# Pooled attention with a top-1 mixture of experts: the first batch's keys loaded and summed another way, score groups on two banks of their own in the first four tiles, weights' low parts on GpSimd, and a new table of order

## The chip, the cores and the metric

The kernel runs on one core of one Trainium2 chip. A core has a matrix engine (PE, TensorE), a vector engine (DVE, VectorE), an activation engine (ACT, ScalarE), GpSimd (POOL), a queue engine that issues most transfers (SP), and 16 DMA engines. Matrix results go to PSUM, which has eight banks of 512 float32 columns on 128 partitions here; everything else lies in SBUF. Each engine takes its instructions strictly in the order in which the program lists them. The metric is the device time of one execution, in microseconds (us).

## The reference

Four batches of 12,288 queries of 128 channels, and four images of 384 x 32 pixels of 128 channels. The image is averaged over 4 x 4 pixels, giving 768 positions, and projected; the result is both key and value. Attention over the 768 keys gives 128 channels per query, and each query then goes through one of eight experts, the one with the greatest gate logit.

```python
kv_pool = kv.reshape(B, H // r, r, W // r, r, C).mean(axis=(2, 4))     # r = 4
k = v = kv_pool.reshape(B, -1, C) @ w_sr
s = 1.0 / np.sqrt(C) * (q @ k.transpose(0, 2, 1))
a = np.exp(s - s.max(-1, keepdims=True))
a /= a.sum(-1, keepdims=True) + 1e-09
x = (a @ v)                                                   # then, per token:
logits = x @ w_gate;  expert_idx = argmax(logits);  gate_w = softmax(logits)[expert_idx]
out = gate_w * (np.maximum(x @ w1[e], 0.0) @ w2[e])           # e = expert_idx
```

## The kernel before, in words

**Tiles.** The 49,152 tokens are cut into 96 tiles of 512 (`T`), 24 per batch (`SPB`). A tile's queries are four groups of 128. Keys are 768 wide (`NK`), six blocks of 128 (`NB`).

**Precision.** Each operand of a large product is split into a high part (a rounded fp32r copy, made by `high` on ACT) and a low part (the rest, made by `low` on DVE or POOL), and `mm3` (lines 218 to 221) adds three products of those parts into one bank. A line number L219, L220 or L221 in the profile is therefore the first, second or third product of any stage, L213 any high part and L216 any low part by a subtraction.

**Keys** (`keys`, from line 242). For each of the six blocks of a batch: `load` brings 1 MB of pixels as two halves of 512 KB into buffers named raw (three of them), `pool` sums each half on DVE (L256), `join` adds the two sums on POOL (L262), `turn` transposes on PE (L267), `mean` scales on ACT, `project` multiplies by w_sr twice (L285, L288), `high_kv` and `low_kv` split the results into kh, vh (ACT) and kl, vl (DVE).

**Attention** (`attention`, from line 675). `turn_q` transposes a tile's queries on DVE (L689), `high_q` and `low_q` split them (qh on ACT, ql on POOL). For each of the four groups: `scores` makes 768 columns with six matmuls, `maxima` reduces them on DVE (nmax, L719), `exps` takes the exponential on ACT (prob, L730). The two sides of the scores alternate and share 1536 columns, that is banks 0, 1 and 2: side 0 has columns 0 to 767, side 1 the next 768, so bank 1 holds the end of the one and the start of the other. In tiles 3 and later prob is transposed on DVE (pb, L742), moved by DMA into pt and split into pth (ACT) and pt (POOL); in tiles 0 to 2 (`FIRST`) PE transposes it (L771), ACT makes the high part (pt) and DVE the low part (pb). `values` is the product with vh and vl into bank 7; xh and xl are its split result.

**Routing.** `route` makes the gate logits (L377, L378), copies their diagonal blocks (lgd) and finds each token's expert with a dozen small DVE instructions. The first tile of a batch chooses, in `pick`, the expert that most of its tokens want; that expert's weights are fetched (`load_weights`) into two raw buffers and split by `cut` into wt: four high parts on ACT, and four low parts, of which the columns 0 to 511 (`c` = 0) go to POOL and the columns 512 to 1023 (`c` = 1) to DVE. All tiles of the batch go through that expert; tokens with another expert are written to lists by indirect DMAs on POOL (`put_row`, L664) and handled near the end (`extra`), where `cut` runs again.

**Experts** (`experts`). Per tile eight times: `first` (xh, xl with wt; a bank from the list of three, 3 to 5), `high_h` (hh, ACT, L863), `low_h` (hlow, DVE, L867), and `second` into bank 6 (`BANK_Y`); then the result is transposed, scaled and put out.

**Order.** The table `AT` gives every step a time in units of a sixteenth of a tile; tile i starts at 16 i. A heap sorts the steps, and each engine's order of instructions is the order in which the sorted steps emit them. Nothing is decided on the chip: an instruction whose input or buffer is late holds up all that stand behind it on its engine. An expert of tile i starts 66 units after the tile, so that four tiles of attention stand before the first expert.

## Time and profile before

| | |
|---|---|
| time, median of 3 runs | 2131.17 us (2130.64 to 2135.87) |
| the profiled execution's own time | 2135.3 us, of which span 2133.2 us |
| PE busy | 2017.7 us, 95% of the span, 9316 matmuls |
| DVE busy | 1636.6 us, 77% |
| ACT busy | 1310.5 us, 61% |
| POOL busy | 1301.8 us, 61% |
| DMA moved | 239.89 MB, mean 112 GB/s |

The page counts the time in which an engine runs an instruction. What matters for an engine near 100% is where it is idle: 2133.2 less 2017.7 leaves 115.5 us in which PE has nothing to do. A row of a group gives count, busy time, mean duration, then the idle time of that engine just before, with the work whose end released it ("<-"). In a timeline, a bracket behind a row is the idle time in front of it. Matmul rows overlap one another (a row lasts longer than the distance to the next), so distances between starts are used for their rate.

### The profile page before, as it was taken

What the parts mean: (1) busy time and instruction counts of PE and PEld (TensorE: products, weight loads), DVE (VectorE), ACT (ScalarE), POOL (GpSimd) and SP (SyncE); (2) the same over time, 40 slices, a digit from 0 to 9 for tenths busy, and PEclk for the clock granted to TensorE, in tenths of its full rate; (3) what the DMA queues carried; (4) which work ended last, traced back from release to release, by engine and by line L of the source; (5) the groups of instructions that cost most, each with busy time, mean ns of one, the idle gap of its engine ahead of it and who ended that gap; (6) DMA issues with size and microseconds to landing.
All of it is one profiled execution on the core that took longest, in us unless ns stands there. A gap on an engine that the chain in (4) does not pass through costs nothing.

```text
span 2133.2 us, 29728 instructions
## 1 busy us (share of the span) xinstructions
PE 2017.7 (95%) x9316; PEld 1654.3 (78%) x9316; DVE 1636.6 (77%) x2658; ACT 1310.5 (61%) x2630; POOL 1301.8 (61%) x1157
## 2 busy tenths in 40 slices
PE   3789999999989999999999999999998999999997
PEld 2568888878868888878877888887886888787885
DVE  5577788987777777988777777888777777778764
ACT  1556666666656666666665666666665666666562
POOL 1044467776676667678677757667767666445541
PEclk9999999999999999999999999999999999999999
DMA  7345546665555455665555455665544554645441
GB/s 136 78 95 118 103 97 135 140 125 125 108 129 116 95 107 115 136 149 120 116 110 122 97 118 100 133 145 129 123 89 107 107 116 93 149 89 129 93 86 21
DMA packets 497651, 239.89 MB, mean 112 GB/s; under 512 B 427441, under 2 KB 433715, under 8 KB 497489
## 3 DMA queue, kind: packets, MB, share of 16 engines
q1 hardware_dynamic: 488144, 237.69, 53.3%
q0 software_dynamic: 9344, 0.26, 0.3%
q8 instruction: 74, 1.21, 0.2%
q14 instruction: 89, 0.72, 0.1%
HBM read 59.97 MB, written 31.92 MB: 43 GB/s over the span
## 4 chain that ended last, share of the span: by engine, by line
PE 78%; DVE 7%; issue 4%; DMA 3%; ACT 3%; POOL 2%; SPq 2%; POOLq 0%; DVEq 0%; ACTq 0%
PE ps L219 25%; PE ps L221 25%; PE ps L220 25%; DVE hlow L867 1%; DVE half L256 1%; DVE nmax L719 1%; ACT prob L730 1%; DMA pt<-pb 1%; SPq L752 1%; PE ps L378 1%; PE ps L377 1%; DVE wt L216 1%; DVE pb L742 1%; DMA raw<-in_kv_dram 1%; DMA raw<-in_moe_w_dram 1%
## 5 line engine op out<-in xcount | busy, mean ns | idle before, releaser
L863 ACT ACTIVATE hh<-ps 128x512 fp32r<-128x512 f32 x768 | 458.5, 597 | 406.7 <-PE ps L221 347.3
L216 POOL TENSOR_TENSOR pt<-pt,pth 128x1024 fp32r<-128x1024 f32 x279 | 668.9, 2414 | 27.3 <-ACT pth L213 24.8
L867 DVE SCALAR_TENSOR_TENSOR hlow<-ps,hh 128x512 fp32r<-128x512 f32 x768 | 518.5, 676 | 171.3 <-ACT hh L863 152.7
L730 ACT ACTIVATE prob<-ps,nmax 128x768 f32<-128x768 f32 x384 | 354.2, 922 | 207.7 <-DVE nmax L719 204.8
L742 DVE STREAM_TRANSPOSE pb<-prob 128x768 f32<-128x768 f32 x372 | 359.8, 967 | 117.4 <-ACT prob L730 111.8
L719 DVE TENSOR_REDUCE nmax<-ps 128x1 f32<-128x768 f32 x384 | 363.9, 948 | 90.5 <-PE ps L221 84.4
L664 POOL DMA_INDIRECT lists<-row,dst x288 | 290.3, 1008 | 61.1 <-issue 54.6
L219 PE MATMUL ps<-xh,wt 128*128 128x512 f32 x768 | 308.3, 401 | 4.8 <-DVE hlow L867 4.6
L219 PE MATMUL ps<-hh,wt 128*128 128x512 f32 x768 | 309.3, 403 | 0.0
L221 PE MATMUL ps<-xh,wt 128*128 128x512 f32 x768 | 306.0, 398 | 0.0
L220 PE MATMUL ps<-xl,wt 128*128 128x512 f32 x768 | 304.6, 397 | 0.0
L221 PE MATMUL ps<-hh,wt 128*128 128x512 f32 x768 | 303.6, 395 | 0.0
L219 PE MATMUL ps<-kh,qh 128*128 128x512 f32 (+1 forms) x768 | 266.9, 348 | 38.6 <-ACT prob L730 37.5
L220 PE MATMUL ps<-hlow,wt 128*128 128x512 f32 x768 | 303.0, 395 | 0.0
L213 ACT CAST pth<-pt 128x1024 fp32r<-128x1024 f32 x279 | 283.3, 1051 | 4.1 <-DMA pt<-pb 4.1
L221 PE MATMUL ps<-kh,ql 128*128 128x512 f32 (+1 forms) x768 | 262.9, 342 | 0.1
L220 PE MATMUL ps<-kl,qh 128*128 128x512 f32 (+1 forms) x768 | 263.0, 342 | 0.0
L216 POOL TENSOR_TENSOR ql<-qt,qh 128x512 fp32r<-128x512 f32 x96 | 124.2, 1294 | 184.7 <-issue 89.2
L220 PE MATMUL ps<-pt,vh 128*128 128x512 f32 x558 | 218.2, 391 | 1.2 <-POOL pt L216 1.1
L221 PE MATMUL ps<-pth,vl 128*128 128x512 f32 x558 | 219.3, 393 | 0.0
L219 PE MATMUL ps<-pth,vh 128*128 128x512 f32 x558 | 219.2, 393 | 0.0
L219 PEld LDWEIGHTS ps<-kh,qh 128*128 128x128 f32 x768 | 147.1, 192 | 71.3 <-ACT prob L730 45.5
(203 smaller groups left out, 2948.6 us busy)
## 6 DMA issues: line engine op xcount, KB each, us to landing
pt<-pb SPq DMA_DIRECT2D x372, 384.0 KB
raw<-in_kv_dram SPq DMA_DIRECT2D x96, 256.0 KB
qb<-in_q_dram SPq DMA_DIRECT2D x384, 64.0 KB
out_dram<-yo SPq DMA_DIRECT2D x384, 64.0 KB
raw<-in_moe_w_dram SPq DMA_DIRECT2D x12, 512.0 KB
lists<-row,dst POOLq DMA_INDIRECT x288, 2.1
kvs<-kh SPq DMA_DIRECT2D x4, 384.0 KB
kvs<-kl SPq DMA_DIRECT2D x4, 384.0 KB
```

Source lines behind the costliest of these rows:

```text
L213: nc.scalar.copy(out=dst, in_=src)
L216: eng.tensor_tensor(out=dst, in0=src, in1=h.bitcast(F32), op=ALU.subtract)
L219: nc.tensor.matmul(out=ps, lhsT=wh, rhs=xh, start=start, stop=False)
L220: nc.tensor.matmul(out=ps, lhsT=wh, rhs=xl, start=False, stop=False)
L221: nc.tensor.matmul(out=ps, lhsT=wl, rhs=xh, start=False, stop=stop)
L256: nc.vector.reduce_sum(out=half, in_=own["raw", kb, h].rearrange("p r (j c) -> p c r j", c=C), axis=AX.XY)
L664: put = nc.gpsimd.indirect_dma_start(out=lists, out_offset=bass.IndirectOffsetOnAxis(ap=state["dst", b, c][:, n : n + 1].bitcast(U32), axi ...
L719: nc.vector.tensor_reduce(out=nmax, in_=own["s", a], op=ALU.max, axis=AX.X, negate=True)
L730: nc.scalar.activation(out=by_key(prob) if i < FIRST else prob, in_=split_keys(own["s", a]) if i < FIRST else own["s", a], func=AF.Exp, bi ...
L742: nc.vector.transpose(out=own["pb"][:, :, :, a, :].rearrange("p c b t -> p b c t"), in_=own["prob", a].rearrange("p (b c t) -> p b c t", c ...
L863: nc.scalar.activation(out=hh, in_=own["hp", f], func=AF.Relu)
L867: nc.vector.scalar_tensor_tensor(out=hl, in0=own["hp", f], scalar=0.0, in1=own["hh", f].bitcast(F32), op0=ALU.max, op1=ALU.subtract,)
```

## The change

1. **Keys of the first batch.** Of the twelve halves of pixels of batch 0, five go to the buffers named pth (four of them, not in use until tile 3) instead of raw, so that seven halves fit at once. They are summed otherwise: `add_rows` adds the second half to the first on DVE (1024 columns), then the second row of that to the first (512 columns); what is left, four pixels side by side, is summed by PE, with four matmuls against the identity that accumulate in one bank (in place of one transpose). The low parts kl and vl come later in the order. Batches 1 to 3 stay as they were.
2. **Scores of tiles 0 to 3** (`HEAD`). A group's 768 columns are two halves of 384 in two banks of their own: banks 0 and 1 for side 0, banks 2 and 6 for side 1. Later tiles keep the shared bank, but side 1 does its private bank's 512 columns first.
3. **`mm3`** does the product with the low part of the stationary operand second and the one with the low part of the moving operand third (before: the other way round).
4. **`cut`** gives all four low parts of the weights to POOL, and the four steps stand 1.05 units apart, starting 3.88 units before `first` (before: 5.08).
5. **Order.** A new table `AT`; tile 0's query steps come 13.19 units earlier; the fill of the lists' pads moves from 4 to 90.

On DVE, in the sums of the first batch's pixels (raw and pth are pixels, half the sums, kl and vl the low parts of a block's keys and values), before:

```order
L256 TENSOR_REDUCE half_184<-raw_169 128x128
L297 SCALAR_TENSOR_TENSOR kl_179<-ps_152,kh_178 128x128
L216 TENSOR_TENSOR vl_181<-ps_152,vh_180 128x128
L256 TENSOR_REDUCE half_190<-raw_172 128x128
L256 TENSOR_REDUCE half_205<-raw_194 128x128
```

and now:

```order
L275 TENSOR_TENSOR raw_165<-raw_165,pth_168 128x1024
L276 TENSOR_TENSOR raw_165<-raw_165 128x512
L318 SCALAR_TENSOR_TENSOR kl_178<-ps_152,kh_177 128x128
L218 TENSOR_TENSOR vl_180<-ps_152,vh_179 128x128
L275 TENSOR_TENSOR pth_189<-pth_189,pth_192 128x1024
L276 TENSOR_TENSOR pth_189<-pth_189 128x512
```

Before, the low parts of the first block stood between the two halves of the second block; now they stand behind the whole second block, so that the sums of a block no longer wait for the block before it to be projected.

On PE, the scores of tile 0, from the end of its first group to the first transposes of prob, with the engines that a row waits for, before:

```order
L219 MATMUL ps_152<-kh_178,qh_299 128x256
L220 MATMUL ps_152<-kl_179,qh_299 128x256 [waits DVE_49]
L221 MATMUL ps_152<-kh_178,ql_301 128x256
L219 MATMUL ps_152<-kh_178,qh_299 128x256 [waits Activation_49]
L220 MATMUL ps_152<-kl_179,qh_299 128x256
L221 MATMUL ps_152<-kh_178,ql_301 128x256
L219 MATMUL ps_152<-kh_178,qh_299 128x512
L220 MATMUL ps_152<-kl_179,qh_299 128x512
L221 MATMUL ps_152<-kh_178,ql_301 128x512
L771 MATMUL ps_152<-ident_79,prob_319 128x128 x6
```

and now:

```order
L221 MATMUL ps_152<-kh_177,qh_266 128x384 [waits Activation_49]
L222 MATMUL ps_152<-kh_177,ql_279 128x384
L223 MATMUL ps_152<-kl_178,qh_266 128x384 [waits DVE_49]
L221 MATMUL ps_152<-kh_177,qh_266 128x384
L222 MATMUL ps_152<-kh_177,ql_279 128x384
L223 MATMUL ps_152<-kl_178,qh_266 128x384
L221 MATMUL ps_152<-kh_177,qh_266 128x384
L222 MATMUL ps_152<-kh_177,ql_279 128x384
L223 MATMUL ps_152<-kl_178,qh_266 128x384
L221 MATMUL ps_152<-kh_177,qh_266 128x384 [waits Activation_49]
L222 MATMUL ps_152<-kh_177,ql_279 128x384
```

The second group waited for ACT (the exponential of the first); now six matmuls of the second group follow with no wait, and the wait for ACT stands in front of the third.

On POOL, where the weights of batch 1 are cut (wt1 the low parts, pt the low parts of prob, lists the indirect DMAs), before:

```order
L461 TENSOR_TENSOR sx_6027<-row_5922,quad_123 128x16
L216 TENSOR_TENSOR wt1_78<-raw_6007,wt1_78 128x512
L664 DMA lists_75<-row_2692,dst_4297 397312x2
L664 DMA lists_75<-row_4573,dst_5872 397312x2
L216 TENSOR_TENSOR pt_5798<-pt_5798,pth_5936 128x4x256
L216 TENSOR_TENSOR wt1_78<-raw_6008,wt1_78 128x512
L216 TENSOR_TENSOR pt_5798<-pt_5798,pth_6014 128x4x256
L664 DMA lists_75<-row_2692,dst_4297 397312x2
L664 DMA lists_75<-row_4573,dst_5872 397312x2
L216 TENSOR_TENSOR pt_5798<-pt_5798,pth_6029 128x4x256
```

and now:

```order
L218 TENSOR_TENSOR pt_5793<-pt_5793,pth_5907 128x4x256
L486 TENSOR_TENSOR sx_6033<-row_5919,quad_123 128x16
L689 DMA lists_75<-row_2689,dst_4291 397312x2
L218 TENSOR_TENSOR wt1_78<-raw_6000,wt1_78 128x512
L689 DMA lists_75<-row_4570,dst_5866 397312x2
L218 TENSOR_TENSOR wt1_78<-raw_6000,wt1_78 128x512
L218 TENSOR_TENSOR wt1_78<-raw_6001,wt1_78 128x512
L218 TENSOR_TENSOR pt_5793<-pt_5793,pth_5966 128x4x256
L218 TENSOR_TENSOR wt1_78<-raw_6001,wt1_78 128x512
L689 DMA lists_75<-row_2689,dst_4291 397312x2
L689 DMA lists_75<-row_4570,dst_5866 397312x2
L218 TENSOR_TENSOR pt_5793<-pt_5793,pth_6017 128x4x256
```

POOL has two weights' parts more between the second and the third low part of prob; the first low part of prob now stands ahead of all of them.

The diff, with the table cut to the entries that the text speaks of:

```diff
 AT = {
...
-    "put": 6.25, "cut": -5.08,
...
+    "put": 9.84, "early_q": -13.19, "cut": -3.88, "cut_step": 1.05,
 }
...
+    HEAD = 4
...
     def mm3(ps, wh, wl, xh, xl, start, stop):
         nc.tensor.matmul(out=ps, lhsT=wh, rhs=xh, start=start, stop=False)
-        nc.tensor.matmul(out=ps, lhsT=wh, rhs=xl, start=False, stop=False)
-        nc.tensor.matmul(out=ps, lhsT=wl, rhs=xh, start=False, stop=stop)
+        nc.tensor.matmul(out=ps, lhsT=wl, rhs=xh, start=False, stop=False)
+        nc.tensor.matmul(out=ps, lhsT=wh, rhs=xl, start=False, stop=stop)
...
         def load(kb):
             for h in range(2):
-                raw = own["raw", kb, h] = kp.tile([P, POOL // 2, POOL * C], F32, name="raw", bufs=3)
+                if b == 0 and (2 * kb + h) % 7 > 2:
+                    raw = ap.tile([P, QT, 2, P], F32R, name="pth", bufs=4).bitcast(F32)
+                    raw = raw.rearrange("p (r a) b c -> p r (a b c)", r=POOL // 2)
+                else:
+                    raw = kp.tile([P, POOL // 2, POOL * C], F32, name="raw", bufs=3)
+                own["raw", kb, h] = raw
...
+        def add_rows(kb):
+            r0, r1 = own["raw", kb, 0], own["raw", kb, 1]
+            nc.vector.tensor_tensor(out=r0, in0=r0, in1=r1, op=ALU.add)
+            nc.vector.tensor_tensor(out=r0[:, 0], in0=r0[:, 0], in1=r0[:, 1], op=ALU.add)
         def turn(kb):
             pt = own["pt", kb] = take()
-            nc.tensor.transpose(out=pt[:, :P], in_=own["pooled", kb], identity=ident)
+            if b:
+                nc.tensor.transpose(out=pt[:, :P], in_=own["pooled", kb], identity=ident)
+                return
+            for j in range(POOL):
+                nc.tensor.matmul(
+                    out=pt[:, :P], lhsT=own["raw", kb, 0][:, 0, j * C : (j + 1) * C], rhs=ident,
+                    start=j == 0, stop=j == POOL - 1,
+                )
...
-                    (0.4, low_kv, kb),
+                    (0.4 if b else 2.0, low_kv, kb),
...
-        low(wt[:, 2 * n + 1, cs], wf[:, cs], wt[:, 2 * n, cs], nc.vector if c else nc.gpsimd)
+        low(wt[:, 2 * n + 1, cs], wf[:, cs], wt[:, 2 * n, cs], nc.gpsimd)
...
-                at(t + 3 * n + 0.8 * c, cut, own, wts[b % 2], n, c)
+                at(t + AT["cut_step"] * (2 * n + c), cut, own, wts[b % 2], n, c)
...
-            own["s", a] = flat[:, side * NK : (side + 1) * NK]
             gs = slice(a * P, (a + 1) * P)
-            cut = NK - T if side else T
-            for hs in (slice(0, cut), slice(cut, NK)):
-                mm3(own["s", a][:, hs], qh[:, gs], ql[:, gs], kh[:, hs], kl[:, hs], True, True)
+            if i < HEAD:
+                s_ps = (ps[:, 2 : BANK_Y + 1 : BANK_Y - 2] if side else ps[:, 0:2])[:, :, :NH]
+                own["s", a] = s_ps
+                parts = [(s_ps[:, h], slice(h * NH, (h + 1) * NH)) for h in range(2)]
+            else:
+                s_ps = own["s", a] = flat[:, side * NK : (side + 1) * NK]
+                cut = NK - T if side else T
+                parts = [(s_ps[:, hs], hs) for hs in (slice(0, cut), slice(cut, NK))]
+                if side:
+                    parts.reverse()
+            for out_ps, hs in parts:
+                mm3(out_ps, qh[:, gs], ql[:, gs], kh[:, hs], kl[:, hs], True, True)
...
-        at(t + AT["turn_q"], turn_q)
+        early = AT["early_q"] if i == 0 else 0.0
+        at(t + AT["turn_q"] + early, turn_q)
...
-    at(4, fill_pads)
+    at(90, fill_pads)
```

More of the change, by code (lines that the diff above doesn't have):

```diff
@@ L100, in tile_pooled_attention_top1_moe @@
     HBP = P // WB
+    QT = P // SQ
     cp = ctx.enter_context(tc.tile_pool(name="const", bufs=1))
@@ L309, in keys @@
         for kb in range(NB):
+            sums = (
+                [(0.5 * step, pool, kb, 0), (0.15 * step, pool, kb, 1), (0.05 * step, join, kb)]
+                if b
+                else [(0.7 * step, add_rows, kb)]
+            )
             series(
                 t + kb * step,
-                [
-                    (0, load, kb), (0.5 * step, pool, kb, 0), (0.15 * step, pool, kb, 1), (0.05 * step, join, kb),
+                [(0, load, kb)] + sums + [
                     (0.5 * step, turn, kb), (0.4, mean, kb), (1.1, project, kb), (0.5, high_kv, kb),
-                    (0.4, low_kv, kb),
+                    (0.4 if b else 2.0, low_kv, kb),
                 ],
@@ L670, in put_row @@
         tc.add_to_no_dep_group("rows", put.ins)
-    QT = P // SQ
     def attention(t, i):
@@ L719, in maxima @@
             nc.vector.tensor_reduce(
-                out=nmax, in_=own["s", a], op=ALU.max, axis=AX.X, negate=True
+                out=nmax, in_=own["s", a], op=ALU.max, axis=AX.XY if i < HEAD else AX.X, negate=True
             )
@@ L729, in exps @@
             k = pj * G + a
+            p_out, s_in = prob, own["s", a]
+            if i < FIRST:
+                p_out = by_key(prob).rearrange("p (h n) c t -> p h n c t", h=2)
+                s_in = s_in.rearrange("p h (n c t) -> p h n c t", t=SQ, c=P // SQ)
+            elif i < HEAD:
+                p_out = prob.rearrange("p (h k) -> p h k", h=2)
             nc.scalar.activation(
-                out=by_key(prob) if i < FIRST else prob,
-                in_=split_keys(own["s", a]) if i < FIRST else own["s", a],
-                func=AF.Exp, bias=own["nmax", a], scale=1.0,
+                out=p_out, in_=s_in, func=AF.Exp, bias=own["nmax", a], scale=1.0,
                 accum_out=grp["sums"][:, k : k + 1],
@@ L770, in turn_first @@
                 a, k = divmod(n * G + c, NB)
+                after("exp", i, a)
                 nc.tensor.transpose(
@@ L781, in low_first @@
             give(own["pp", n])
+            done("first_p", i, n)
         def values(k):
@@ L793, in values @@
                 after("low_p", i, k // 2)
+            else:
+                for n in range(NB):
+                    after("first_p", i, n)
             if i < FIRST:
```

24 lines of the change are left out of this document (12 added, 12 removed).

## The prediction

> **What bounds the kernel now.** I read the page's span first, then busy time by stretch (columns: stretch, its length, then PE, PEld, DVE, ACT and POOL busy with instruction counts, the granted PE clock, the DMA engines' busy share, GB/s), then PE's waits (total us, times, longest).
>
> ```profile
> span 2133.2 us, 29728 instructions
> ```
>
> ```profile
> 0.00:42.70 42.70, 10.24 (x30) 6.71 (x30) 26.92 (x34) 6.79 (x20) 7.26 (x40) 1.00 0.64 167
> 42.70:128.00 85.30, 61.11 (x249) 46.57 (x250) 45.56 (x79) 42.80 (x79) 9.69 (x10) 0.93 0.44 65
> 128.00:600.00 472.00, 469.17 (x2177) 387.21 (x2176) 378.41 (x604) 305.71 (x614) 303.90 (x259) 0.99 0.57 119
> 600.00:630.00 30.00, 21.54 (x89) 15.97 (x88) 24.88 (x41) 15.39 (x32) 24.13 (x22) 0.94 0.63 143
> 1100.00:1133.00 33.00, 24.16 (x93) 17.73 (x92) 25.24 (x41) 14.54 (x31) 25.82 (x24) 0.84 0.59 141
> 1605.00:1637.00 32.00, 23.45 (x97) 17.49 (x97) 26.42 (x43) 15.67 (x32) 25.89 (x23) 0.95 0.50 112
> ```
>
> PE is full between the starts of batches (469.17 of 472.00 us), so there nothing can be won or hidden: only PE's own idle time counts. It lies in three places: 42.70 - 10.24 = 32.5 us while the first keys are made, 85.30 - 61.11 = 24.2 us in the first four tiles, and 8.46, 8.84 and 8.55 us where batches 1, 2 and 3 begin. The change touches all three.
>
> **Part 1, the first keys.** Timeline of DVE (start, us, idle before and releaser), then the chain of waits (start, us):
>
> ```profile
> 6.31 1.87 DVE L256 TENSOR_REDUCE half<-raw 128x128 f32<-128x1024 f32 x1 [6.31 <-DMA raw<-in_kv_dram]
> 8.74 1.87 DVE L256 TENSOR_REDUCE half<-raw 128x128 f32<-128x1024 f32 x1 [0.56 <-DMA raw<-in_kv_dram]
> ```
>
> ```profile
> 14.39 1.79 DVE half L256
> 16.25 0.46 POOL pooled L262
> 16.76 0.49 PE ps L267
> 17.72 0.81 PE ps L285 x2
> 18.53 0.44 PE ps L288 x2
> 19.95 1.79 DVE half L256
> ```
>
> A block takes 19.95 - 14.39 = 5.56 us because everything is one ring: the second half's sum, the join, the transpose, the mean (the gap to 17.72), two products, and then DVE makes this block's low parts before it may sum the next half. The change opens the ring (low parts stand one block later), drops the join, and frees the transfers from waiting for the sums. Three things can then set the pace.
>
> Transfers: the stretch 0 to 42.70 shows 167 GB/s at a busy share of 0.64, so 261 GB/s if never idle. After the second half (8.7 us) ten halves of 0.524 MB and tile 0's queries (0.26 MB) follow: 5.5 MB, 21 us, the last at 29.8 us. At the pace of the first two (8.74 - 6.31 = 2.43 us a half) it is 8.7 + 10 x 2.43 + 1 = 34.0.
>
> PE: a product of this kind costs 0.81 us, the next behind it 0.44, so four take 0.81 + 3 x 0.44 = 2.1 instead of 0.49; with 0.5 for the mean and 1.25 for the projections a block holds PE 3.85 us, and six from 10.6 us on end at 33.7.
>
> DVE: no addition of two SBUF tensors of 1024 columns is in this trace. The reductions it replaces bound it above (3.74 us a block); below, half of that. The nearest row is the weights' low part of 512 columns from two SBUF tensors:
>
> ```profile
> 121.87 0.68 DVE L216 TENSOR_TENSOR wt<-raw,wt 128x512 fp32r<-128x512 f32 x1
> ```
>
> It gives 2 x 0.68 + 0.68 = 2.0 us a block, hidden under a transfer pace of 4 us; only the last block's shows.
>
> I take the transfers: 29.8 + 2.0 (sums) + 2.1 + 0.5 + 1.25 + 0.5 (high parts) = 36.2 for the first scores, which now start at 42.7 (the end of the first stretch above): **-6.5 us**, between -2.4 (34.0 instead of 29.8) and -8 (PE's pace). SP's 24 issues of pixels, now in one row ahead of the queries of tiles 1 to 4, do not hold: about 0.6 us each is 14 us. The pads' transfer, moved behind them, is wanted by no one before the lists.
>
> **Part 2, tiles 0 to 3.** PE's timeline at its second group of scores, its waits in the stretch 42.70 to 128, and three durations from the chain of waits:
>
> ```profile
> 48.19 0.58 PE L219 MATMUL ps<-kh,qh 128*128 128x256 f32 x1 [2.69 <-ACT prob L730]
> ```
>
> ```profile
> PE ps L219 <- ACT prob L730: 19.6, 12, 4.2
> ```
>
> ```profile
> 50.59 0.97 DVE nmax L719
> ...
> 55.85 0.87 PE ps L771 x4
> 56.72 0.02 issue
> 56.74 0.58 ACT pt L213
> ```
>
> The second group had its own columns, yet PE waited 2.69 us for the exponential of the first: the two share bank 1. Twelve such waits make 19.6 of the 24.2 us. With four banks a group waits only for the exponential two groups back. What then sets the pace is ACT's order. Its timeline, four of the exponentials:
>
> ```profile
> 46.53 1.60 ACT L730 ACTIVATE prob<-ps,nmax 128x768 f32<-128x768 f32 x1 [3.87 <-DVE nmax L719]
> ...
> 71.71 1.66 ACT L730 ACTIVATE prob<-ps,nmax 128x768 f32<-128x768 f32 x1 [3.00 <-DVE nmax L719]
> ...
> 89.93 1.65 ACT L730 ACTIVATE prob<-ps,nmax 128x768 f32<-128x768 f32 x1 [2.06 <-DVE se L446]
> ...
> 123.59 0.90 ACT L730 ACTIVATE prob<-ps,nmax 128x768 f32<-128x768 f32 x1 [3.54 <-DVE nmax L719]
> ```
>
> They are group 0 of tile 0, group 1 of tiles 1 and 2, and group 0 of tile 4: steps of 25.2, 18.2 and 33.7 us, 77.1 in all. By the new order:
> - Tile 0 to 1: the second group's scores follow the first's at once, and its exponential the first's after 1.9 us (six matmuls of 384 columns at the half rate below). From there exponential 1.6, four transposes 0.87, three casts 1.75, exponentials 1.6 and 1.6, transposes 0.87, two casts 1.2, exponential 1.6, cast 0.58, low part 0.7, nmax 0.97, that is 13.3, and some 12 hand-overs of 0.1: 14.6. Together 16.5 against 25.2, -8.7.
> - Tile 1 to 2: the routing of tile 0 (a dozen small DVE rows and their exponential) stands in this step, before and now; I take no gain.
> - Tile 2 to 4: a tile's step is 14.6 plus the casts for xh and the logits' copies (1.6), less twice 0.7 for exponentials of 0.90 instead of 1.60: 14.8; the three groups left are three quarters of that, 11.1, and the weights' casts 1.2. Together 27.1 against 33.7, -6.6, of which about 2 are the low parts on DVE that stand before tile 4's nmax and go.
>
> That is -15.3. A sum of rows leaves out collisions that it does not see, so I take **-13**; the bounds are -6 (the wait of 2.69, the 2 of the low parts and little of the rest) and -19.6 (all twelve waits).
>
> The half rate:
>
> ```profile
> 71.04 0.42 PE ps L220
> 71.46 0.23 PE ps L221
> ```
>
> Until 71.4 us a product of 512 columns took 0.42 us, then 0.23. The Trainium skill (TensorE: Matmul & The Clock Gate, Part 1) says that the array runs at half rate until it has been kept busy for about 3.4 us; the change would by that rule reach the full rate inside tile 0, and its transposes would be some 1.5 us shorter than the sum has them: 2093.5 instead of 2095 by that estimate. The sum keeps the half rate.
>
> **Part 3, the starts of batches 1 to 3.** Timelines of DVE, POOL, PE:
>
> ```profile
> 617.46 5.45 DVE L216 TENSOR_TENSOR wt<-raw,wt 128x512 fp32r<-128x512 f32 x1
> ```
>
> ```profile
> 612.45 1.28 POOL L216 TENSOR_TENSOR wt<-raw,wt 128x512 fp32r<-128x512 f32 x1 [2.97 <-ACT wt L213]
> ...
> 618.76 1.30 POOL L216 TENSOR_TENSOR wt<-raw,wt 128x512 fp32r<-128x512 f32 x1
> 620.00 2.35 POOL L216 TENSOR_TENSOR pt<-pt,pth 128x1024 fp32r<-128x1024 f32 x1
> ```
>
> ```profile
> 624.86 0.58 PE L219 MATMUL ps<-kh,qh 128*128 128x256 f32 x1 [4.55 <-ACT prob L730]
> ```
>
> The same subtraction that took 0.68 us takes 5.45 here. It ends at 622.91, just after POOL's run of SBUF work (to 622.35): DVE stood blocked while POOL worked back to back. The nmax behind it was late, so were the exponential and the scores, and PE stood for 4.55 us. The other two starts idle alike (8.84 and 8.55 us), and the clock of all three is below 1 (0.94, 0.84, 0.95). The change takes this subtraction off DVE. I count 4.55, plus 1.5 for the clock (about 0.05 of 30 us), less 0.5 for what is late next: 5.5 each, **-16.5**. Bounds: 0 (first rival) and -22.5 (7.5 each, some of the smaller waits of the same stretch too).
>
> The price is on POOL: two more parts of 1.30 us per batch, with the low parts of prob, the queries', the scaling of outputs and the lists' transfers queued behind. From the first weight part, the second low part of prob ended 622.35 - 612.45 = 9.9 us later, behind two weight parts, four list transfers and the first low part. By the new order there stand three weight parts and one list transfer ahead of it, and the first low part has gone before: by the rows and about 1 us for a list transfer 3 x 1.3 + 1 + 2.4 = 7.3. It is no later, and the third, behind one weight part more and the same two list transfers, is not either. So I cost this at nothing. The head's four cuts on POOL, 5.2 us, delay the first tile's `second`, not its `first`; POOL is all but idle there (9.69 of 85.30).
>
> **The rest** of the table (and `mm3`'s order: as many loads and matmuls) leaves the full stretches full: 0. The cuts near the end: 0.
>
> **Sum.** The profiled execution took 2135.3 us (span 2133.2, 2.1 around it), 4.1 above the median. 2135.3 - 6.5 - 13 - 16.5 = 2099.3; against the median 2131.2 - 36 = **2095 us**.
>
> **Rivals.**
> - *POOL takes DVE's place at the starts* (0.12). POOL is busy 24.13 of 30.00 us there; 2.6 more in a stretch shortened by 6 leaves none free, and a low part of prob late by 5 us stops PE as long. Against it: the running sums above. Part 3 is then 0: 2131.2 - 19.5 = 2112. The Trainium skill (Perfetto Trace Analysis, Optimizing Scalar/DVE Operations) says that moving work between GpSimd and DVE might not help, since they share an SBUF read port; by that, this would be the outcome, 2112. The 5.45 us row shows the sharing, but also that it is DVE's loss that PE feels.
> - *The head gives its lower bounds* (0.12, a quarter of it together with the first): pixels at 2.43 us a half, and ACT, DVE and routing in place of the bank: 2131.2 - 2.4 - 6 - 16.5 = 2106.
> - *Slower* (0.05): in every full tile the new order puts one exponential ahead of an expert's ReLU:
>
> ```profile
> 272.62 0.60 ACT L863 ACTIVATE hh<-ps 128x512 fp32r<-128x512 f32 x1 [1.00 <-PE ps L221]
> ```
>
> ```profile
> 276.25 0.39 PE L219 MATMUL ps<-xh,wt 128*128 128x512 f32 x1
> ```
>
> ACT is free for 1.00 us before that ReLU, and an exponential takes 0.90. If its nmax is late, the ReLU and hlow are too, and with them the bank that a later `first` waits for. The bank is wanted again at about 276.25, so the slack is 276.25 less the ReLU's end (273.2) less about 0.7 for hlow: 2.3 us. Beyond that each 0.1 us costs 91 x 0.1 = 9 us. Half a microsecond too much: 2095 + 45 = 2140. Against it: on PE the scores for that exponential now stand one product stage (0.7 us) earlier.
>
> **How the numbers follow.** Forecast 0.71, the rivals as given. Low end 2083: the forecast's own bounds all at their best would be 2081. High end 2114: it takes in both faster rivals. A measurement of this kernel tells about 0.3% (6.4 us) from no change. All but the slower rival and mishaps added up lie more than that below 2131: faster 0.91, same 0.04, slower 0.05.
>
> **What would show it.** First scores near 36 us, and pixel transfers without gaps until 30; no wait of 2 to 3 us for prob in front of a tile's second group; tile 4's first exponential near 104 us (123.59 - 19.5); no wait above 3 us at the three starts, and no DVE row of 5 us. Wrong, if POOL's low part of prob releases PE at the starts, or if the full stretches show PE idle.

## The result and the profile after

The changed kernel takes 2071.2 us (median of 4 runs, 2068.5 to 2071.7) against 2131.6 before: a ratio of 0.971, 95% interval 0.9693 to 0.9727. I had forecast 2095 with a range of 2083 to 2114: the direction was right, the gain was 60 us instead of 36, and the time lies below the range.

The page's span after, and busy time by stretch (stretch, length, then PE, PEld, DVE, ACT, POOL busy with counts, granted clock, DMA share, GB/s). The stretches are cut at events that both traces have: first scores, tile 0's and tile 4's first exponential, and those of tiles 12, 36, 60 and 84, so that each of the middle rows holds one start of a batch:

```profile
span 2070.0 us, 29923 instructions
```

```profile
0.00:33.96 33.96, 17.53 (x73) 14.94 (x73) 16.46 (x32) 6.36 (x18) 6.85 (x35) 1.00 0.81 211
...
36.69:97.95 61.26, 48.12 (x229) 40.27 (x230) 38.82 (x71) 40.81 (x76) 8.14 (x9) 0.89 0.39 72
...
254.64:747.78 493.14, 488.82 (x2273) 402.97 (x2272) 400.38 (x648) 324.70 (x648) 355.19 (x307) 1.00 0.58 121
...
1737.05:2070.00 332.95, 314.45 (x1514) 260.49 (x1512) 226.84 (x404) 198.11 (x392) 158.65 (x145) 0.98 0.45 98
```

The same of the kernel before, for two stretches that the prediction does not show:

```profile
282.41:784.74 502.33, 491.78 (x2273) 404.35 (x2272) 404.42 (x650) 320.95 (x648) 351.48 (x305) 0.99 0.57 119
...
1791.58:2133.20 341.62, 317.02 (x1514) 261.29 (x1512) 232.06 (x408) 196.81 (x392) 156.36 (x142) 0.98 0.44 96
```

| stretch between the same events | before | after | gain | forecast |
|---|---|---|---|---|
| start to first scores | 42.71 | 33.96 | 8.7 | 6.5 |
| first scores to tile 0's first exponential | 3.82 | 2.73 | 1.1 | 0 |
| on to tile 4's first exponential | 77.06 | 61.26 | 15.8 | 13 |
| tile 4 to 12 | 158.82 | 156.69 | 2.1 | 0 |
| tile 12 to 36 (start of batch 1) | 502.33 | 493.14 | 9.2 | 5.5 |
| tile 36 to 60 (start of batch 2) | 504.44 | 494.70 | 9.7 | 5.5 |
| tile 60 to 84 (start of batch 3) | 502.40 | 494.57 | 7.8 | 5.5 |
| tile 84 to the end (late extra rounds) | 341.62 | 332.95 | 8.7 | 0 |

The gains add up to the 63.2 us between the two spans. Every term was too small, and three rows had been put at nothing. How the gain divides over the first three rows changes by some 2 us from one execution to another: in two other profiles with the same first tiles (cut_starts and ql_later below) first scores come at 35.3 us and the third row takes 58.8, and tile 4's first exponential comes at 97.4, against 97.95 here. Of the 9.2 us around batch 1, PE's idle time gave 6.2 (502.33 - 491.78 = 10.55, now 4.32) and its busy time 3.0.

What is left at a start of a batch, from DVE's, POOL's and PE's timelines of the changed kernel (start, us, idle before and releaser):

```profile
573.02 1.84 DVE L533 TENSOR_TENSOR oh<-chosen,order 128x32 f32<-128x32 f32 x1
```

```profile
573.52 1.28 POOL L218 TENSOR_TENSOR ql<-qt,qh 128x512 fp32r<-128x512 f32 x1
```

```profile
575.16 0.17 PE L546 MATMUL ps<-tot,ones 128*128 128x8 bf16 x1 [2.29 <-DVE tot L541]
```

PE's waits of 0.6, 0.7, 0.6 and 4.6 us are gone; the wait for the count behind the first pick of experts (2.00 before) is left.

### The profile page after: what moved, and what is told of

The parts are those of the page before. It is cut to its first block, busy times and chain, and to the rows that moved or that the text cites. A ratio compares the mean times of both kernels' runs of the same rounds, so it can differ in the third digit from the quotient of the medians.

```text
span 2070.0 us, 29923 instructions
## 1 busy us (share of the span) xinstructions
PE 2008.7 (97%) x9358; PEld 1657.5 (80%) x9358; DVE 1605.3 (78%) x2646; ACT 1323.6 (64%) x2630; POOL 1317.9 (64%) x1163
## 3 DMA queue, kind: packets, MB, share of 16 engines
q8 instruction: 75, 1.23, 0.2%
## 4 chain that ended last, share of the span: by engine, by line
PE 87%; DVE 6%; DMA 2%; SPq 1%; issue 1%; ACT 1%; POOL 1%; DVEq 0%; POOLq 0%; ACTq 0%
PE ps L221 28%; PE ps L223 28%; PE ps L222 28%; DVE hlow L909 1%; DVE nmax L751 1%; PE ps L403 1%; PE ps L402 1%; DVE pb L778 1%; SPq L788 1%; ACT prob L768 1%; DVE half L264 1%; PE ps L306 0%; PE ps L808 0%; SPq L258 0%; DMA pt<-pb 0%
## 5 line engine op out<-in xcount | busy, mean ns | idle before, releaser
L215 ACT CAST pth<-pt 128x1024 fp32r<-128x1024 f32 x279 | 291.8, 1046 | 16.0 <-DMA pt<-pb 14.6
L221 PE MATMUL ps<-kh,qh 128*128 128x256 f32 (+2 forms) x768 | 260.9, 340 | 3.3 <-ACT prob L768 3.1
L223 PE MATMUL ps<-kl,qh 128*128 128x256 f32 (+2 forms) x768 | 260.1, 339 | 0.0
L222 PE MATMUL ps<-kh,ql 128*128 128x256 f32 (+2 forms) x768 | 260.0, 339 | 0.0
L937 POOL TENSOR_TENSOR yo<-yb,sb 128x512 f32<-128x512 f32 x96 | 101.0, 1052 | 221.6 <-issue 109.3
```

Source lines behind the costliest of these rows:

```text
L215: nc.scalar.copy(out=dst, in_=src)
L221: nc.tensor.matmul(out=ps, lhsT=wh, rhs=xh, start=start, stop=False)
L222: nc.tensor.matmul(out=ps, lhsT=wl, rhs=xh, start=False, stop=False)
L223: nc.tensor.matmul(out=ps, lhsT=wh, rhs=xl, start=False, stop=stop)
L937: nc.gpsimd.tensor_tensor(out=own["yo"], in0=own["yb"].rearrange("p (n d) -> p n d", d=SQ), in1=sb.unsqueeze(2).broadcast_to([P, G * G, SQ ...
```

## Experiments: the first keys

Six of the twelve halves of pixels, not five, go to the buffers named pth: the page of the profile counts 12 transfers of 256 KB into them, two for a half. Three runs split Part 1 into its loads and its sums. The first has all of it as before:

```diff
-                if b == 0 and (2 * kb + h) % 7 > 2:
+                if False:
...
-            if b:
+            if True:
                 nc.tensor.transpose(out=pt[:, :P], in_=own["pooled", kb], identity=ident)
                 return
...
             sums = (
                 [(0.5 * step, pool, kb, 0), (0.15 * step, pool, kb, 1), (0.05 * step, join, kb)]
-                if b
+                if True
                 else [(0.7 * step, add_rows, kb)]
             )
...
-                    (0.4 if b else 2.0, low_kv, kb),
+                    (0.4, low_kv, kb),
...
-        early = AT["early_q"] if i == 0 else 0.0
+        early = 0.0
```

> The changed kernel with the first batch's keys made as before: pixels loaded into three buffers, summed by DVE's reductions, joined on GpSimd, turned by one transpose, low parts in the same block, and tile 0's queries turned where the others are. Theory 1: the 8.75 us by which the first scores came earlier go, and the 1.1 us that the first exponential won on top (the first scores run at the half rate again): 2080 to 2082 us, first scores near 42.7 us, a product of 384 columns at 0.3 us or more in tile 0. Theory 2: the tiles behind swallow part of it, since weights, lists or later queries set their pace and not the keys: 2074 to 2078. Theory 3: the half rate then lasts through the first tiles, as it did in the kernel before until 71 us, and costs more: 2084 to 2088.

Measured: 2082.5 us (2079.0 to 2083.3), 11 more than the changed kernel; first scores at 42.77. The whole loss is in the head: the time from tile 0's to tile 4's first exponential is 60.5 us, against 61.3 after.

> The changed kernel with the first batch's pixels loaded into three buffers instead of seven, so that a transfer waits until a block before it is summed; the sums stay half on TensorE. Theory 1: transfers set the pace, and a wait for a buffer adds to each block: first scores 3 to 6 us later, 2075 to 2079 us. Theory 2: the sums on TensorE free the buffers early enough: 2070 to 2073 us. Theory 3: as slow as the old keys: 2080 us or more.

Here only the first edit of the diff above is made (three raw buffers). Measured: 2079.8 us (2076.4 to 2082.0), and first scores as late as with the old keys, 8.8 us later than after where theory 1 had 3 to 6. DVE's and PE's timelines:

```profile
25.63 1.23 DVE L275 TENSOR_TENSOR raw<-raw 128x1024 f32<-128x1024 f32 x1 [3.43 <-DMA raw<-in_kv_dram]
```

```profile
42.78 0.67 PE L221 MATMUL ps<-kh,qh 128*128 128x384 f32 x1
```

DVE waits 3.4 us for pixels that could not be sent for until a buffer was free.

> The changed kernel with the first batch's sums as before (two reductions of 1024 columns on DVE, a join on GpSimd, one transpose on TensorE), while its pixels are still loaded at once into seven buffers and low parts still stand a block late. With sums and loads both as before the kernel took 2082.5 us. Theory 1, mine: the transfers set the pace and the ring is opened by the loads, so the sums are hidden: first scores at 36 to 38 us, 2071 to 2075 us. Theory 2: DVE becomes the pace (two reductions of 1.95, two low parts of 0.28 and tile 0's turn: 4.5 a block from 6.3 us on, 33.5 for the last half's sum): first scores at 36.5 to 39 us and 2074 to 2078 us. Theory 3: the ring itself is what the sums cost (join and hand-overs): near 42 us, 2080 us or more.

Here only the sums are as before (the two `if True` of the diff). Measured: 2072.1 us (2069.2 to 2073.4), first scores at 35.65, from PE's timeline:

```profile
35.65 0.67 PE L221 MATMUL ps<-kh,qh 128*128 128x384 f32 x1
```

In the profiles of all kernels with the new keys they lie between 33.96 and 36.16, so the half of the sums that went to TensorE is worth nothing that can be told. The loads are what counts, as theory 1 said. Two smaller parts were not taken alone: the low parts' later place and tile 0's earlier queries, which the last two runs both keep.

## Experiments: tiles 0 to 3

The banks without the order, then the order without the banks:

```diff
-    HEAD = 4
+    HEAD = 0
...
-                p_out = by_key(prob).rearrange("p (h n) c t -> p h n c t", h=2)
-                s_in = s_in.rearrange("p h (n c t) -> p h n c t", t=SQ, c=P // SQ)
+                p_out, s_in = by_key(prob), split_keys(s_in)
```

> The changed kernel with the score groups of the first four tiles on three banks that share one, as all other tiles have them. Theory 1: the four banks made all of the 15.8 us that the change won between tile 0's first exponential and tile 4's (77.1 to 61.3), less about 2 that came from the weights' low parts: 2084 to 2087 us, with PE waiting 2 us or more for prob before a tile's second and fourth group. Theory 2: the new order of exponentials and casts in these tiles made half of it: 2077 to 2080 us.

```diff
-    ("first_p", 0): 8.67, ("first_p", 1): 5.16, ("first_p", 2): 4.44, ("first_p", 3): 8.51, ("first_p", 4): 5.05,
-    ("first_p", 5): 5.87, "first_high": 0.8, "first_low": 1.23, "first_values": 2.54,
+    ("first_p", 0): 6.32, ("first_p", 1): 4.1, ("first_p", 2): 4.74, ("first_p", 3): 5.1, ("first_p", 4): 5.32,
+    ("first_p", 5): 7.4, "first_high": 0.5, "first_low": 1.3, "first_values": 2.69,
```

> The changed kernel with the old times of the first three tiles' turns of prob, their casts, low parts and value products (first_p, first_high, first_low, first_values); the four banks stay. The run without the banks took 69.2 us from tile 0's first exponential to tile 4's, against 61.3 with them and 77.1 before, so half of what was won there is not the banks'. Theory 1: it is this order: 67 to 70 us for that stretch, 2077 to 2081 us in all. Theory 2: it is the earlier full rate of TensorE, the weights' low parts off DVE and other things, which stay: 61 to 63 us for the stretch, 2069 to 2073 us.

Measured: 2081.1 us without the banks (2080.1 to 2083.1), 2089.0 with the banks and the old order (2085.7 to 2091.7). The stretch between the two exponentials, of the first and of the second kernel, with a wait of PE from each:

```profile
38.24:107.41 69.17, 51.69 (x233) 40.60 (x233) 39.41 (x71) 41.26 (x76) 8.16 (x9) 0.84 0.32 63
```

```profile
43.71 0.58 PE L221 MATMUL ps<-kh,qh 128*128 128x256 f32 x1 [2.48 <-ACT prob L767]
```

```profile
39.46:115.59 76.13, 51.88 (x233) 42.19 (x231) 40.46 (x70) 41.17 (x75) 9.24 (x9) 0.86 0.28 59
```

```profile
42.58 1.97 PE L808 MATMUL ps<-ident,prob 128*128 128x128 f32 x8 [2.81 <-ACT prob L768]
```

So the stretch takes 77.1 us before, 76.1 with the banks and the old order, 69.2 with the new order and the shared bank, and 61.3 with both. The banks alone are worth at most about 1 us; the kernel before with nothing changed but the weights' low parts (before_pool below) shows 76.2 here too. PE, which takes its work in order, stands before the transposes of a prob that is not there, 2.81 us instead of 2.69 before the scores. Theory 1 of the second run had the place right and the size wrong (76 instead of 67 to 70); theory 2 of the first is nearer than theory 1.

## Experiments: the starts of batches

One step tells these runs apart: the time from tile 24's to tile 32's first exponential, with the start of batch 1 in it. It is 172.7 us before and 164.7 after.

First, the cut alone, in both directions:

```diff
-        low(wt[:, 2 * n + 1, cs], wf[:, cs], wt[:, 2 * n, cs], nc.gpsimd)
+        low(wt[:, 2 * n + 1, cs], wf[:, cs], wt[:, 2 * n, cs], nc.vector if c and own.get("batch") else nc.gpsimd)
```

> The changed kernel, but with the weights' second low part of each pair (columns 512 to 1023) back on DVE where a batch begins; the two late extra rounds keep it on GpSimd, and all times and orders of the change stay. Theory 1: what the change won at the three starts (8.8 to 9.8 us each between the same exponentials of the two traces, 26.8 in all) is won by taking this subtraction off DVE; then DVE shows a row of 3 us or more at each start and the kernel takes 2093 to 2098 us. Theory 2: only the one wait behind the 5.45 us row comes back, 3 x 4.55 us: 2085. Theory 3: the new times of the other steps, or the wider spacing of the cuts, did it: 2069 to 2074, no DVE row above 1.5 us.

In the kernel before:

```diff
-        low(wt[:, 2 * n + 1, cs], wf[:, cs], wt[:, 2 * n, cs], nc.vector if c else nc.gpsimd)
+        low(wt[:, 2 * n + 1, cs], wf[:, cs], wt[:, 2 * n, cs], nc.gpsimd)
```

> The kernel before with one edit: all low parts of the weights on GpSimd. Theory 1 (the subtraction on DVE is the whole cost of the starts): 26.8 us less at the starts, 2 to 4 at the end, about 2 at the first tiles: 2098 to 2102 us. Theory 2 (the wait behind the long row alone): 3 x 4.55 = 13.7, and the same smaller terms: 2111 to 2115. Theory 3 (GpSimd then is late with prob's low parts in the old order, and the new times were needed for it): 2125 or more, with PE waiting for GpSimd's pt at the starts.

Measured: 2072.5 us (2071.5 to 2073.5) with DVE's subtraction back at the starts of the changed kernel, step 164.7; 2115.4 (2113.1 to 2116.5) for the kernel before with every part on GpSimd, step 169.3. The first of them, DVE's timeline:

```profile
585.95 0.94 DVE L751 TENSOR_REDUCE nmax<-ps 128x1 f32<-128x768 f32 x1
586.81 3.11 DVE L218 TENSOR_TENSOR wt<-raw,wt 128x512 fp32r<-128x512 f32 x1
```

DVE is held for 3.1 us and nobody waits: the row maxima of the score group stand ahead of the held row now, behind it before. My reason, that the starts gain because the subtraction leaves DVE, is not needed here. In the second run PE's stall changes its releaser:

```profile
618.22 0.50 PE L220 MATMUL ps<-pt,vh 128*128 128x512 f32 x1 [3.06 <-POOL pt L216]
```

That is the first rival, POOL in DVE's place, in the old order, and it takes back a part: the step is 3.4 us shorter instead of 8.0. So the other new times were taken one by one. The old cut (engine and times) in the changed kernel; then the old times of prob's casts and low parts as well; then all old times but the cut's and the first tiles'; then the new times of prob's casts and low parts in the kernel before:

```diff
-    "put": 9.84, "early_q": -13.19, "cut": -3.88, "cut_step": 1.05,
+    "put": 9.84, "early_q": -13.19, "cut": -5.08, "cut_step": 1.05,
...
-                at(t + AT["cut_step"] * (2 * n + c), cut, own, wts[b % 2], n, c)
+                at(t + 3 * n + 0.8 * c, cut, own, wts[b % 2], n, c)
...
-        low(wt[:, 2 * n + 1, cs], wf[:, cs], wt[:, 2 * n, cs], nc.gpsimd)
+        low(wt[:, 2 * n + 1, cs], wf[:, cs], wt[:, 2 * n, cs], nc.vector if c else nc.gpsimd)
```

> The changed kernel with the weights' cut as it was: second low part of each pair on DVE (starts and late rounds), at the old times (-5.08, parts 0.8 and pairs 3 apart). All other new times stay. The run with DVE's part back at the starts alone lost nothing (2072.5 us), the one with it back in the late rounds lost 16. Theory 1: where the cut's rows stand in DVE's order decides (behind the old one the row maxima of a score group waited, ahead of the new one they are through): the starts' 26.8 us come back, with the late rounds' 16: 2108 to 2116 us. Theory 2: the new times of the other steps did it: the late rounds' 16 alone, 2085 to 2090 us.

```diff
-    ("high_p", 0): 23.35, ("high_p", 1): 26.36, ("high_p", 2): 28.89, "low_p": 6.59,
+    ("high_p", 0): 24.51, ("high_p", 1): 27.68, ("high_p", 2): 28.78, "low_p": 6.6,
```

> The changed kernel with the weights' cut as it was (the second low parts on DVE, the old times; 2089.5 us) and with the old times of prob's casts and low parts too (high_p, low_p). In the run with the old cut alone, GpSimd made prob's first low part ahead of the lists' transfers, and DVE's second subtraction then fell beside those transfers and took 0.67 us. Theory 1: this place of prob's low part is what cured the starts: with it taken back, DVE's subtraction falls beside low part, weights' part and low part, takes 5 us or more, and the 24 us that the starts had won go for the most part: 2105 to 2115 us. Theory 2: other times did it (scores, values, expert products): 2086 to 2093 us, DVE's row below 1.5 us.

The third run has the new cut, and in the table (some of the entries):

```diff
-    "high_q": -9.56, "exps": 1.9, ("scores", 3): 12.21, ("high_p", 0): 23.35, ("values", 3): 40.72, "apart": 5.66,
+    "high_q": -7.6, "exps": 2.04, ("scores", 3): 12.5, ("high_p", 0): 24.51, ("values", 3): 39.33, "apart": 4.33,
...
-    ("first", 5): 74.3, "scale_y": 2.2, "put": 9.84,
+    ("first", 5): 74.05, "scale_y": 1.03, "put": 6.25,
```

> The changed kernel with the old times of every step that both tables have, apart from the first tiles' turns of prob (first_p and their casts) and the cut, which keep the new ones. Theory 1: the cut's engine and times alone made the starts faster: 2069 to 2075 us. Theory 2: the new times of the other steps carry part of it, as in the kernel before with all low parts on GpSimd, where PE waited 3.06 us for prob's low part at the starts: 3 x 3 us and some at the late rounds, 2080 to 2088 us. Theory 3: all of it, starts and late rounds: 2098 us or more.

The last has the diff of prob's entries above turned round, in the kernel before:

> The kernel before with one part of the new table: the new times of prob's casts and low parts (high_p, low_p). DVE's order stays as it was; on GpSimd prob's first low part comes ahead of the lists' transfers, so that DVE's second subtraction of the weights should fall beside these transfers. Theory 1: that alone cures the starts of batches as well as moving the subtraction off DVE does: no DVE row of the weights above 2 us at the three starts, 6 to 8 us less for each (tile 24 to 32: 165 to 167 us instead of 172.7), 2107 to 2114 us in all. Theory 2: it cures them only together with other new times: the row stays above 4 us, 2128 us or more.

| kernel | median, us | step, tile 24 to 32 | weights' second row on DVE |
|---|---|---|---|
| before | 2131.6 | 172.7 | 5.45 |
| before, all parts on GpSimd | 2115.4 | 169.3 | none |
| before, prob's low part early | 2141.5 (2140.6 to 2146.2) | 167.7 | 0.66 |
| changed, old cut | 2089.5 (2088.3 to 2091.7) | 165.1 | 0.67 |
| changed, old cut, prob's low part late | 2139.0 (2136.4 to 2141.6) | 173.7 | 5.84 |
| changed, other times old | 2078.9 (2076.2 to 2082.0) | 165.8 | none |
| changed | 2071.2 | 164.7 | none |

POOL's and DVE's timelines with the old cut, prob's low part early:

```profile
586.21 2.86 POOL L218 TENSOR_TENSOR pt<-pt,pth 128x1024 fp32r<-128x1024 f32 x1
589.39 1.01 POOL L689 DMA_INDIRECT lists<-row,dst  x1
```

```profile
589.98 0.67 DVE L218 TENSOR_TENSOR wt<-raw,wt 128x512 fp32r<-128x512 f32 x1
```

and with the low part late again:

```profile
597.08 2.39 POOL L218 TENSOR_TENSOR pt<-pt,pth 128x1024 fp32r<-128x1024 f32 x1
599.40 1.30 POOL L218 TENSOR_TENSOR wt<-raw,wt 128x512 fp32r<-128x512 f32 x1
600.65 2.36 POOL L218 TENSOR_TENSOR pt<-pt,pth 128x1024 fp32r<-128x1024 f32 x1
```

```profile
597.73 5.84 DVE L218 TENSOR_TENSOR wt<-raw,wt 128x512 fp32r<-128x512 f32 x1
```

The same subtraction takes 0.67 us beside a list transfer and 5.84 beside three rows of GpSimd on SBUF. So the starts have two cures, each of which gives nearly all: prob's low part ahead of the list transfers on POOL (165.1), or the cut off DVE at its new times (165.8). The change has both (164.7). Prob's low part early does most of it in the kernel before too (167.7, where theory 1 of the last run had 165 to 167 for the step).

For the whole kernel that run came out on the other side of its expectation, 2141.5, and the one with the low part late came out 24 us above its own. In both, moving prob's entries of the table without the others has a price elsewhere. PE's waits in the middle of a batch, of the kernel before with prob's low part early, and of the changed kernel with it late:

```profile
452.50 0.17 PE L612 MATMUL ps<-xtot,upper 128*128 128x8 bf16 x1 [4.20 <-DVE xtot L607]
```

```profile
433.48 0.80 PE L221 MATMUL ps<-xh,wt 128*128 128x512 f32 x1 [4.20 <-DVE hlow L909]
```

The first was 1.78 us in the kernel before: prob's low part now stands ahead of the lists' own steps on POOL. In front of the second, DVE stands 5.62 us for another step of the lists on POOL (pos, L661), which has two of prob's low parts and a list transfer ahead of it, and the rows of hlow stand behind DVE's.

## Experiments: what holds a DVE row

```diff
-        low(wt[:, 2 * n + 1, cs], wf[:, cs], wt[:, 2 * n, cs], nc.vector if c else nc.gpsimd)
+        if c:
+            nc.vector.tensor_copy(out=wt[:, 2 * n + 1, cs], in_=wf[:, cs])
+        else:
+            low(wt[:, 2 * n + 1, cs], wf[:, cs], wt[:, 2 * n, cs], nc.gpsimd)
```

> The kernel before, with DVE's low part of the weights' second halves replaced by a plain copy of the weights on DVE at the same place: one SBUF operand is read instead of two, so the expert products take in a wrong low part for those columns. In the traces DVE's transposes, reductions and subtractions from PSUM take the same time whether GpSimd works beside them or not (0.98 and 0.96 us for a transpose of 768 columns), and rows with two SBUF operands do not (0.19 and 1.83 us for one of 32 columns). Theory 1: it is the second SBUF operand: the copy takes 0.7 us or less at the three starts, and the 4.55 us waits go: 2112 to 2119 us. Theory 2: any DVE row of this size that writes SBUF beside GpSimd is held: a row of 3 us or more, 2128 us or more.

Measured: 2128.4 us (2124.7 to 2132.0). Theory 1 falls; the copies, from DVE's timeline:

```profile
611.82 0.43 DVE L340 CAST wt<-raw 128x512 fp32r<-128x512 f32 x1 [1.76 <-DMA raw<-in_moe_w_dram]
...
615.96 6.47 DVE L340 CAST wt<-raw 128x512 fp32r<-128x512 f32 x1
```

The copy has one SBUF operand and is held as long; alone it takes 0.43 us, less than the 0.68 of the subtraction. Other rows on DVE show the same time beside GpSimd's arithmetic as alone (medians in the kernel before): the transpose of prob 0.94 and 0.98 us, the row maxima 0.96 and 0.96, the subtraction for xl, which reads PSUM, 0.69 and 0.69. The Trainium skill (SBUF — State Buffer, Who interferes with whom) says that DVE and GpSimd contend for one pair of SBUF ports when DVE has two SBUF inputs, or copies in a mode that uses both ports, and that reductions never do. The rows agree: the subtraction and the copy are held, the reductions are not; in which mode the copy ran, no trace tells. It also says that the loser waits until the other instruction is finished; here it waited through three that stood back to back on GpSimd.

The 2.29 us that are left at a start are then the same thing: `oh`, two SBUF operands of 32 columns, 1.84 us beside GpSimd's `ql`. One exchange of neighbours on POOL tests it; a second run also moves the lists' counts:

```diff
-        at(t + AT["low_q"] + early, low_q)
+        at(t + AT["low_q"] + early + (2.5 if b and s == 4 else 0.0), low_q)
```

> The changed kernel with one low part of queries on GpSimd (the tile four behind a batch's first, where the batch's experts are picked) put behind the two list transfers that follow it; on GpSimd two neighbours change places three times, and no other engine's order changes. In the changed kernel DVE's comparison of 32 columns from two SBUF operands takes 1.84, 1.83 and 1.83 us there, beside that low part, against 0.19 in batch 0, and PE waits 2.29, 2.41 and 2.29 us for what comes of it. Theory 1: GpSimd's work on SBUF holds DVE's row: 0.2 us for the row, PE's waits down to 0.7, 3 x 1.65 = 5 us less than the changed kernel in the same call. Theory 2: the row is held by the list transfers or its own input: it stays at 1.8 us and the time within 1.5 us of the changed kernel's.

```diff
-            ... (0.6, totals), (0.6, ranks), (0.3, places),
+            ... (0.6, totals), (2.2 if c == 1 else 0.6, ranks), (0.3, places),
```

> As the run before it, and in the middle of each batch's lists TensorE's two counting products stand one expert stage later, since PE waits up to 1.88 us for their input there (6.2 us in four places). Theory 1: these waits go too, and 8 to 10 us are won over the changed kernel. Theory 2: the steps behind the counts, on DVE and GpSimd, come later with them and fall beside prob's low parts, so that as much is lost as won: within 2 us of the run before it, or above the changed kernel.

> The changed kernel itself, beside the two runs of this call: 2068 to 2073 us.

Measured side by side: 2063.5 us (2061.0 to 2067.4), ratio to the kernel before 0.9684 (0.9669 to 0.9699); with the counts moved too 2064.6 (2063.7 to 2065.4); the changed kernel again 2072.5 (2069.1 to 2076.7), 0.972 (0.9702 to 0.9738). The first, DVE's and PE's timelines:

```profile
572.53 0.19 DVE L533 TENSOR_TENSOR oh<-chosen,order 128x32 f32<-128x32 f32 x1
```

```profile
573.02 0.17 PE L546 MATMUL ps<-tot,ones 128*128 128x8 bf16 x1 [0.65 <-DVE chosen L446]
```

Theory 1 held, with more than its price: this version is 8.9 us faster than the changed kernel, and the three waits shrank by 4.9 in all. The counts moved later bring nothing more, as theory 2 of that run said: their waits fall from 1.88 to 1.1 and PE waits about 1 us for prob's low part at each start instead.

A part of the rest is in the clock column behind the wait; the changed kernel beside it, then the version with `ql` later:

```profile
575.70:580.00 4.30, 4.28 (x13) 3.37 (x13) 3.38 (x8) 2.87 (x6) 3.98 (x3) 0.60 0.22 56
```

```profile
573.00:577.00 4.00, 3.98 (x20) 3.31 (x20) 3.07 (x8) 3.13 (x7) 3.52 (x5) 1.00 0.12 20
```

After a wait of 2.29 us eight products start 0.43 us apart instead of 0.23, 1.6 us; after 0.65 none does. Wait and clock together show in the steps at the three starts (tile 24 to 32 and its likes), which are 2.2, 2.1 and 2.2 us shorter, 6.5 in all. The two profiles also differ by 3.1 us where the edit does nothing: behind two waits of 1.88 us for the lists' count, which both kernels have, the changed kernel lost the full rate and this one did not (tile 44 to 48 takes 82.9 and 81.3 us, tile 68 to 72 82.9 and 81.4). So it is not shown that all of the 8.9 comes from the exchange.

## Experiments: the late rounds

The cut's line as in the first diff on the starts, with `nc.vector if c and "batch" not in own`:

> The changed kernel, but with the weights' second low part back on DVE in the two late extra rounds alone. Between the same exponentials of the two traces the change won 8.7 us behind 1790 us, which I had costed at nothing. Theory 1: all of it comes from this subtraction: 2079 to 2081 us. Theory 2: only the three waits of PE for hlow that the old trace shows there come from it (1.29, 0.91 and 1.42 us, 3.6 in all), and the rest from the gathered rows, which PE waited 2.55 and 2.20 us for and now 0 and 1.29: 2074 to 2076. Theory 3: nothing of it, the new times did it: 2070 to 2072.

Measured: 2087.3 us (2084.8 to 2089.3), 16 more than the changed kernel and nearly twice what theory 1 had. DVE's and PE's timelines:

```profile
1793.42 2.44 DVE L218 TENSOR_TENSOR wt<-raw,wt 128x512 fp32r<-128x512 f32 x1 [2.79 <-ACT wt L215]
```

```profile
1797.63 0.79 PE L221 MATMUL ps<-xh,wt 128*128 128x512 f32 x1 [3.70 <-DVE hlow L909]
```

From tile 84 on the kernel takes 341.6 us before, 346.8 in this run and 333.0 after. DVE first stands 2.79 us for ACT's high part of the weights, is then held at its own row, and hlow stands behind both. With the old engine the new times would have lost 5 us here; GpSimd making the second low parts won 13.9. In the old order the same move won 4.9 (336.8 us in before_pool).

## Why the prediction was right and wrong

Of the 27 us by which the terms fell short of the 63.2, the three starts make 10.2, the late rounds 8.7, the rows put at nothing ahead of tile 12 3.2, Part 2 2.8 and Part 1 2.2.

- **Part 1** ("I take the transfers"): right in its mechanism, and the runs show that the loads make it and the sums do not. -6.5 was -8.7 to the first scores in the profiled execution, and -6.6 at the least in the others with the new keys. Of the sum's links, DVE's additions took 1.23 + 0.69 = 1.92 us in a block (2.0 estimated), but 2.9 in the last, the only one that shows, where the second stood beside GpSimd's `ql` (1.65). Three were too long: the last pixels were there by 28.6 us (29.8), the first scores wait for no high parts (0.5), and PE was at its full rate by the last block, eight products in 1.16 us instead of 2.05. The last is luck of the execution: it came in four of the eleven profiles with the new loads and sums.
- **Part 2**: the row sum said 16.5, 18.2 and 27.1 us, 61.8 together, -15.3; measured 15.6, 16.3 and 29.4, 61.3. The step that failed is the discount, "a sum of rows leaves out collisions that it does not see, so I take -13". The agreement is partly luck: the sum "keeps the half rate", but PE's busy time in the stretch fell from 55.1 to 48.1. And "with four banks a group waits only for the exponential two groups back" is half of the cause: without the new times of the transposes the banks bring 1 us.
- **Part 3**, the largest miss: "I count 4.55, plus 1.5 for the clock, less 0.5" against 9.2, 9.7 and 7.8. The other waits of the same stretch went too (0.59, 0.71 and 0.56 in batch 1), which I had put into the upper bound only, and nothing was late in their place. The reason given, that the subtraction leaves DVE, is one of two cures. I had written down the other one, the early low part of prob, but only as the reason why POOL costs nothing. The clock's 1.5 has the size by which PE's busy time fell (3.0, 1.7 and 1.5), but hardly its cause, since the wait of 2.29 us that is left brings a stretch at the half rate of its own; what shortened the busy time stays open.
- **"The cuts near the end: 0"** was an edit costed at nothing without a named cover: 8.7 us.
- **"The rest leaves the full stretches full: 0"** held: of the 4.32 us in which PE idles between tiles 12 and 36, two waits make 4.2 (1.88 for the lists' count, 2.29 for the pick). The rival with the ReLU did not come. The first rival came only in the old order (3.06 us for POOL's pt); the page of the Trainium skill that I cited for it (Perfetto Trace Analysis, Optimizing Scalar/DVE Operations) says that such a move might not help. Here it did: alone, in the old order, it won 16 us (2115.4), and in the late rounds of the new order 13.9. No run takes the new order of `mm3` or the later pads alone.
- The sentence on the clock gate (2093.5) pointed the right way, and in four of eleven profiles the full rate came earlier still, within the keys; in the others it came in tile 0's scores or later (from 38.7 us on in cut_starts).

## What to carry to other kernels

Where two engines hold each other up, ask which rows stand beside each other and not only which engine does the work: an exchange of neighbours on GpSimd at three places made a version 9 us faster, of which 6.5 show at these places; the new way of loading the first keys won as much. A row that is held costs only what stands behind it and is waited for; look for the consumer before pricing the hold. When a stall has several small companions in the same stretch, its cure can take them all: here the longest wait was 4.55 us, the stretch's idle time 8.5 to 8.8, and the gain 7.8 to 9.7.

## What was not expected of the hardware

- A wait of PE can cost its full rate for 3.4 us behind it. In 18 profiled executions, from 130 us on, I counted the products of 512 columns among the 13 rows after a wait that start about 0.43 us apart instead of 0.23. Of 57 waits of 0.72 to 1.67 us none was followed by four or more; of 79 between 1.67 and 2.21 us 42 were; of 74 longer ones 65, and of the 52 among these that stayed below 3 us 44. The same wait of 1.88 us in the same program lost it at two places and kept it at a third. The Trainium skill (TensorE: Matmul & The Clock Gate, Why this matters for your kernels) advises against gaps above about 3 us; here gaps from 1.7 us on were enough about every second time. Part 1 of that page says that the window which decides runs freely, and this does agree.
- A list transfer's issue on GpSimd (1.0 us) does not hold DVE's subtraction (0.67 us beside it); a low part or a weights' part on GpSimd does.
